# One stretch of attention products per tile in a linear-attention, GLU and expert kernel, with the routing's counting products ahead of every third one

## The chip, the cores and the metric

The kernel runs on one core of one Trainium2 chip. The metric is the device time of one execution in microseconds (us). PE is TensorE, DVE is VectorE, ACT is ScalarE, POOL is GpSimd, SP is SyncE.

## What is computed

Three layers follow one another over 3072 tokens (4 sequences of 768) of 384 columns, all in float32: linear attention with 8 heads of 48 columns and a decay per column, a gated unit (GLU) behind a norm, and a layer of 8 experts of which each token takes one.

```python
def _attn_ref(q, k, v, alpha):                     # [4, 8, 768, 48]
    state = np.zeros((B, H, D, D), dtype=np.float32)
    for t in range(S):
        state = alpha[:, :, t, :, None] * state + np.einsum('bhd,bhe->bhde', k[:, :, t], v[:, :, t])
        y[:, :, t] = np.einsum('bhd,bhde->bhe', q[:, :, t], state)
...
def _moe_ref(x, w_gate, w_val, w_out, rms_g):      # d_ff = 1536
    xn = x / np.sqrt(np.mean(x * x, axis=-1, keepdims=True) + 1e-06) * rms_g
    g = xn @ w_gate
    return (g * (1.0 / (1.0 + np.exp(-g))) * (xn @ w_val)) @ w_out
...
def _moe2_ref(x, w_gate, w_output_gate, w1, w2):   # 8 experts, F = 1024
    logits = x @ w_gate
    e_idx = np.argmax(logits, axis=1)
...
        out[mask] = gate_w[mask, None] * eom[mask, e, None] * (np.maximum(x[mask] @ w1[e], 0.0) @ w2[e])
```

## The kernel before

**Tiles and groups.** The tokens are cut into 24 tiles of 128. Tiles 0 to 17 take turns over the first three sequences, 18 to 23 are the fourth sequence; tiles 15, 16, 17 and 23 are the last of their sequence and have no state product, and 18 is the first of its own: it has no product with an older state. Three tiles make a group g of the GLU, eight groups in all.

**The GLU** runs per group over 12 chunks j of 128 hidden columns, in slots: gate (`m_gate`, L635), val (`m_val`, L654) and, one chunk behind, out (`m_out`, L676), nine matmuls each, since every float32 product is made of three. ACT and DVE work between them: `tt` is the activated gate times val (L661; it frees val's bank of PSUM), `hh` its rounded part (L664, ACT), `hl` the rest (L670, DVE). The next slots of the out kind need `hh` and `hl`.

**Attention of one tile** has five stages (`stages`, L415): score (L430, two banks `ps_s`, for even and for odd heads; behind it DVE makes the masked P, L440, and decays the state, L434), k turned, output (L464 with the older state `wide`, L468 with P), state (L489; DVE adds it to the state, L496), x turned. From tile 9 on (`DT`) it is `moved(t)` (L910) that arranges them: the turns of k and x go through DVE transposes (L557, L510) and DMAs in place of PE, and PE has two visits per tile, the score, and two slots' groups later output and state together (`yd_`, L918). A stage is called behind a slot by `stage()` (L951), when the condition at L1287 says that it is due. What a tile needs ahead of its score (transposes of alpha, k and q, two scans, two multiplications) is its preparation, `prework(t)` (L366), which is queued in `prep` and taken a step per slot.

**The banks.** The attention and the routing take their PSUM banks from one pool, `psA`, with three buffers (L160); the slots have five others. `bank()` (L231) takes the next buffer of the pool, and PE waits until the one that it held last is read.

**The normed output.** ACT squares the output and sums it (L474), POOL makes the scale `ss` of the sum (L475, L476), ACT scales (`xn`, L477), DVE turns it (`xb`, L510).

**Routing** of a group's 384 tokens to experts has two halves: `route_a` (L709), some twenty small operations, mostly DVE's, and `route_b` (L744), six small bf16 products that count tokens per expert (`ps_r`, L748 to L752), a few DVE operations (the two that read the counts are L760 and L767), and three scatters of rows to the experts' buckets, issued by POOL (L769). They are called at fixed slots of the next group, L1292 to L1297.

**What sets the order.** On PE the groups 2 to 6 run in program order (`seq`, L215). The other engines' instructions are put in order by a scheduler at build time, save for the few that are pinned. Each engine works through its own list in that order.

The preparation begins at stage 0 of a tile, ahead of its score:

```python
        if done % NST == 0:
            while prep:
                prep_step()
            if nprep < NTILE and done != GS - NST:
                prep.extend(prework(nprep))
                nprep += 1
```

## Time and profile before

| | before |
|---|---|
| median of 3 runs | 822.46 us (822.12 to 822.76) |
| the profiled execution, its own time | 821.73 us |
| its span | 819.9 us |
| PE, busy | 804.4 us (98%) |
| VectorE, busy | 539.0 us (66%) |
| ScalarE, busy | 326.3 us (40%) |
| POOL, busy | 153.8 us (19%) |
| mean granted clock of TensorE | 0.998 |

The rows come from one profiled execution. Its span is the time from the first to the last instruction in the trace; 1.83 us lie around it, and its own time is 0.73 us below the median of the runs. In the rows, the start of a PE instruction is the number to use: durations of matmuls overlap, so that what a matmul takes is the time from its start to the next one's. The same holds in a smaller degree for VectorE. Times in brackets at a row's end are idle time of that engine ahead of it, and what ended it.

### The profile page before, as it was taken

Reading aid. Unit: us, or ns where it says so; the run is one execution under the profiler, and the core shown is the slowest. Engines: PE = TensorE matmul, PEld = TensorE weight load, DVE = VectorE, ACT = ScalarE, POOL = GpSimd, SP = SyncE. Lnnn points to the kernel's source line nnn. Section 1 sums busy time; section 2 is a strip of 40 time slices with the busy share of each in tenths; the row PEclk is TensorE's granted clock in tenths of the full one; section 3 lists DMA queues with packets and bytes.
Section 4 is the critical chain, followed back from the end, with each engine's and each line's share of the span. In section 5 each row is a group of like instructions: output and inputs, shape, how many; then the busy total and the mean of one; then the engine's idle time right before and its main releaser. Section 6 shows DMA issues by size and latency. Waiting matters only on the chain.

```text
span 819.9 us, 15933 instructions
## 1 busy us (share of the span) xinstructions
PE 804.4 (98%) x5967; PEld 772.2 (94%) x5967; DVE 539.0 (66%) x1202; ACT 326.3 (40%) x694; POOL 153.8 (19%) x207
## 2 busy tenths in 40 slices
PE   7999999999999999999999999999999999999996
PEld 5799999999999999999999999999999999999996
DVE  7998999498677876766776663243357555566631
ACT  1745554333333333422433332325226445554441
POOL 3001000000300020010020001001224325544441
PEclk9999999999999999999999999999999999999999
DMA  9955463773544453334444221005037786778620
GB/s 202 208 155 144 153 170 111 219 181 84 149 111 102 108 137 82 83 97 93 108 119 101 49 47 49 20 9 195 1 116 203 201 223 186 218 233 254 177 86 27
DMA packets 195454, 106.85 MB, mean 130 GB/s; under 512 B 125868, under 2 KB 190122, under 8 KB 195376
## 3 DMA queue, kind: packets, MB, share of 16 engines
q1 hardware_dynamic: 190912, 96.35, 46.1%
q0 software_dynamic: 4464, 9.48, 3.4%
q8 instruction: 47, 0.77, 0.4%
q14 instruction: 31, 0.25, 0.1%
HBM read 80.88 MB, written 25.18 MB: 129 GB/s over the span
## 4 chain that ended last, share of the span: by engine, by line
PE 94%; issue 2%; DVE 1%; DMA 1%; POOL 1%; ACT 0%; POOLq 0%; DVEq 0%; ACTq 0%; SPq 0%
PE ps_o L684 19%; PE ps_g L650 19%; PE ps_v L650 18%; PE ps_h L650 12%; PE ps_b L1196 8%; PE ps_b L1202 4%; PE ps_s L430 3%; PE ps_y L468 3%; PE ps_y L464 2%; PE ps_st L489 1%; PE pc L615 1%; PE ps_n L283 1%; PE junk L860 1%; PE ps_k L450 1%; DMA er<-bucket 0%
## 5 line engine op out<-in xcount | busy, mean ns | idle before, releaser
L664 ACT ACTIVATE hh<-tt 128x384 fp32r<-128x384 f32 x96 | 50.4, 525 | 145.3 <-DVE tt L661 134.8
L661 DVE TENSOR_TENSOR tt<-tt,ps_v 128x384 f32<-128x384 f32 x96 | 52.8, 550 | 82.2 <-PE ps_v L650 69.5
L1176 DVE SCALAR_TENSOR_TENSOR h<-ps_h,h 128x256 fp32r<-128x256 f32 (+6 forms) x72 | 38.1, 532 | 63.5 <-ACT h L1175 60.3
L642 ACT ACTIVATE tt<-ps_g 128x384 f32<-128x384 f32 x96 | 46.9, 488 | 82.8 <-PE ps_g L650 76.9
L670 DVE TENSOR_TENSOR hl<-tt,hh 128x384 fp32r<-128x384 f32 x96 | 54.2, 565 | 24.1 <-ACT hh L664 22.6
L650 PE MATMUL ps_g<-xh,wgh 128*128 128x384 f32 x192 | 66.5, 346 | 0.0
L650 PE MATMUL ps_v<-xh,wvh 128*128 128x384 f32 x192 | 66.4, 346 | 0.0
L684 PE MATMUL ps_o<-wol,hh 128*128 128x400 f32 x192 | 66.3, 345 | 0.0
L650 PE MATMUL ps_g<-xl,wgh 128*128 128x384 f32 x192 | 64.6, 337 | 0.8 <-DVE begin L317 0.8
L684 PE MATMUL ps_o<-woh,hh 128*128 128x400 f32 x192 | 65.3, 349 | 0.0
L650 PE MATMUL ps_v<-xh,wvl 128*128 128x384 f32 x192 | 64.8, 338 | 0.0
L650 PE MATMUL ps_g<-xh,wgl 128*128 128x384 f32 x192 | 64.6, 337 | 0.0
L650 PE MATMUL ps_v<-xl,wvh 128*128 128x384 f32 x192 | 64.5, 336 | 0.0
L684 PE MATMUL ps_o<-woh,hl 128*128 128x400 f32 x192 | 64.0, 345 | 0.0
L1175 ACT ACTIVATE h<-ps_h 128x256 fp32r<-128x256 f32 (+6 forms) x72 | 33.5, 468 | 71.6 <-PE ps_h L650 69.9
L650 PE MATMUL ps_h<-x,w1b 128*128 128x456 f32 (+3 forms) x288 | 57.5, 342 | 0.0
L650 PE MATMUL ps_h<-x,w1a 128*128 128x256 f32 (+3 forms) x288 | 52.2, 325 | 0.0
L650 PEld LDWEIGHTS ps_h<-x,w1b 128*128 128x128 f32 x288 | 50.6, 188 | 1.7 <-ACT x L1156 0.2
L650 PEld LDWEIGHTS ps_h<-x,w1a 128*128 128x128 f32 x288 | 47.2, 188 | 1.0 <-issue 0.3
L440 DVE TENSOR_TENSOR P<-ps_s,mask 128x512 f32<-128x512 f32 x46 | 30.1, 685 | 23.8 <-PE ps_s L430 23.8
L475 POOL TENSOR_SCALAR ss<-ss 128x1 f32<-128x1 f32 x24 | 9.8, 410 | 186.4 <-ACT xn L474 183.1
L1196 PE MATMUL ps_b<-h,w2b 128*128 128x456 f32 (+2 forms) x216 | 43.6, 344 | 0.3 <-ACT h L1175 0.3
(312 smaller groups left out, 2027.3 us busy)
## 6 DMA issues: line engine op xcount, KB each, us to landing
st<-in_moe_w_dram SPq DMA_DIRECT2D x46, 384.0 KB
bucket<-zero SPq DMA_DIRECT2D x8, 772.0 KB
stg<-in_moe_w_gate_dram SPq DMA_DIRECT2D x12, 384.0 KB
stg<-in_moe_w_val_dram SPq DMA_DIRECT2D x12, 384.0 KB
stg<-in_moe_w_out_dram SPq DMA_DIRECT2D x12, 384.0 KB
v<-in_v_dram SPq DMA_DIRECT2D x23, 192.0 KB
more<-in_moe_w_dram SPq DMA_DIRECT2D x9, 384.0 KB
er<-in_moe_w_dram SPq DMA_DIRECT2D x9, 384.0 KB
```

The source lines that it names most:

```text
L430: seq(nc.tensor.matmul(ps[hh][:, p, :], lhsT=kT[r, p, :], rhs=qT[r, p, :], start=True, stop=True))
L440: pace(f'Ph{t}', nc.vector.tensor_tensor(out=Ph, in0=ps[hh], in1=mb, op=ALU.mult))
L642: nc.scalar.activation(tt, ps, AF.Silu)
L650: seq(nc.tensor.matmul(ps, lhsT=a_[:, kc, :], rhs=b_[:, kc, :], start=(n == 0), stop=(n == 3 * KD - 1)))
L661: nc.vector.tensor_tensor(out=tt, in0=tt, in1=ps, op=ALU.mult)
L664: nc.scalar.activation(hh, tt, AF.Copy)
L670: nc.vector.tensor_tensor(out=hl, in0=tt, in1=f(hh), op=ALU.subtract)
L684: seq(nc.tensor.matmul(obank[s][i], lhsT=a_[:, sl], rhs=weight(b_, j), start=(j == j0 and n == 0), stop=(j == j1 - 1 and n == 2)))
L1175: nc.scalar.activation(hh[:, 0, :], ps, AF.Relu)
L1176: nc.vector.scalar_tensor_tensor(out=hh[:, 1, :], in0=ps, scalar=0.0, in1=f(hh[:, 0, :]), op0=ALU.max, op1=ALU.subtract)
L1196: nc.tensor.matmul(ob2[u][k_][:, 0:r * n], lhsT=we[p][b_][:, j, k_ * P:k_ * P + P], rhs=hh[:, a_, :], start=(j == 0 and m == 0), stop=(j = ...
L1202: ins = nc.tensor.matmul(ob2[u][i][0:r], lhsT=hh[:, a_, sl], rhs=we[p][b_][:, j, :], start=(j == 0 and m == 0), stop=(j == KF2 - 1 and m = ...
```

## The change

From tile 9 on the state's products come first, then the output's, and behind them, in the same stage, the score of the next tile, whose `stages` are made there (`scored`). What is left of the next tile's preparation is issued ahead of that. The score stage of these tiles is empty (`no_`), save for tile 9, whose score still stands alone. A tile's preparation is queued one stage earlier, at the last stage of the tile before it.

The second half of the routing, up to group 5, is called directly ahead of such a stretch, at the first one behind its first half: at the tiles 10, 11, 14, 17, 20 and 23. Its two reads of the counts (`counts`) stand ahead of the arithmetic of the gates. The first half lies at slot 4 (group 0), 15 (group 1) or 12 of the next group, where it lay at 1 and 7. Groups 6 and 7 are as before.

```diff
@@ -752,19 +752,26 @@
         seq(nc.tensor.matmul(ps[:, GT, :], lhsT=ones_b, rhs=ohc[:, GT - 1, :], start=True, stop=True))
         bc = [P, GT, E]
 
+        rk = small("rk", bc)
+
+        def counts():
+            nc.vector.tensor_tensor(out=rk, in0=ps[:, 0:GT, :], in1=cnt.to_broadcast(bc), op=ALU.add)
+            nc.vector.tensor_tensor(out=cnt[:, 0, :], in0=cnt[:, 0, :], in1=ps[:, GT, :], op=ALU.add)
+
+        if g < NG - 1:
+            counts()
         nc.vector.tensor_scalar(out=se, in0=se, scalar1=1e-9, scalar2=2.0, op0=ALU.add, op1=ALU.mult)
         nc.vector.reciprocal(out=se, in_=se)
         nc.vector.scalar_tensor_tensor(out=R[:, :, DM:DM + 1], in0=og, scalar=1.0, in1=se, op0=ALU.add, op1=ALU.mult)
         nc.vector.tensor_copy(R[:, :, DM + 1:DM + 2], tokid[:, g * GT:g * GT + GT, :])
-        rk = small("rk", bc)
-        nc.vector.tensor_tensor(out=rk, in0=ps[:, 0:GT, :], in1=cnt.to_broadcast(bc), op=ALU.add)
+        if g == NG - 1:
+            counts()
         nc.vector.tensor_tensor(out=rk, in0=rk, in1=oh, op=ALU.mult)
         pf = small("pf", [P, GT, 1])
         nc.vector.tensor_reduce(out=pf, in_=rk, op=ALU.add, axis=AX.X)
         nc.vector.tensor_scalar(out=m8, in0=m8, scalar1=-float(REG), scalar2=float(E * REG), op0=ALU.mult, op1=ALU.add)
         pos = small("pos", [P, GT, 1], I32)
         nc.vector.tensor_tensor(out=pos, in0=pf, in1=m8, op=ALU.add)
-        nc.vector.tensor_tensor(out=cnt[:, 0, :], in0=cnt[:, 0, :], in1=ps[:, GT, :], op=ALU.add)
         for i in range(GT):
             nc.gpsimd.indirect_dma_start(out=bucket_of[g * GT + i], out_offset=OFF(ap=pos[:, i, 0:1], axis=0),
                                          in_=R[:, i, 0:RW], in_offset=None)
@@ -907,8 +914,10 @@
     DT = CFG['DT']
     laid = []
 
+    scored = {}
+
     def moved(t):
-        s_, k_, y_, d_, _ = stages(t)
+        s_, k_, y_, d_, _ = scored.pop(t) if t in scored else stages(t)
 
         def second():
             if t == DT:
@@ -916,7 +925,12 @@
             return laid.pop() if laid else None
 
         def yd_():
-            posts = [y_(), d_()]
+            posts = [d_(), y_()]
+            if t + 1 < NTILE:
+                while prep:
+                    prep_step()
+                scored[t + 1] = list(stages(t + 1))
+                posts.append(scored[t + 1][0]())
 
             def post():
                 for p in posts:
@@ -934,7 +948,7 @@
 
         def no_():
             return None
-        return s_, second, yd_, turns, no_
+        return s_ if t == DT else no_, second, yd_, turns, no_
 
     def rest():
         yield lambda: None
@@ -950,12 +964,14 @@
 
     def stage():
         nonlocal done, nprep
-        if done % NST == 0:
+        t_, i_ = divmod(done, NST)
+        t_ += GT
+        if i_ == 0 and t_ <= DT:
             while prep:
                 prep_step()
-            if nprep < NTILE and done != GS - NST:
-                prep.extend(prework(nprep))
-                nprep += 1
+        if nprep < NTILE and ((i_ == 0 and t_ < DT and done != GS - NST) or (i_ == NST - 1 and t_ >= DT - 1)):
+            prep.extend(prework(nprep))
+            nprep += 1
         done += 1
         return next(att_stream)()
 
@@ -1285,15 +1301,18 @@
             if post:
                 post()
             if done < (NTILE - GT) * NST + 2 and ((g - 1) * 3 * KF + n + 1 + lead(g, n)) * GT >= (done + 1 - GT * NST) * 3 * KF / NST:
+                if done % NST == 2 and not last:
+                    for g_ in [*rt]:
+                        route_b(g_)
                 post = stage()
                 if post:
                     post()
             prep_step()
-            if g == 2 and n in (1, 3):
-                (route_a, route_b)[n // 2](0)
-            if n == CFG['RA']:
+            if g == 2 and n == 4:
+                route_a(0)
+            if n == (CFG['RA'] if last else 15 if g == 2 else 12):
                 route_a(g - 1)
-            if n == CFG['RB']:
+            if last and n == CFG['RB']:
                 route_b(g - 1)
             if last:
                 if n == 9:
```

On PE, around the output of tile 12, before: output (`ps_y`), state (`ps_st`), then an out slot.

```order
L650 MATMUL ps_v<-xl,wvhe 128x384
L650 MATMUL ps_v<-xh,wvle 128x384
L464 MATMUL ps_y<-wide_127,qT 64x96 x8
L468 MATMUL ps_y<-v,P_3321 64x48 x8
L468 MATMUL ps_y<-v,P_3323 64x48 x8
L489 MATMUL ps_st<-v,kn 64x48 x8
L684 MATMUL ps_o<-wohe,hh 128x400
L684 MATMUL ps_o<-wole,hh 128x400
```

The score of tile 13 stood alone, between a val and an out slot further on:

```order
L650 MATMUL ps_v<-xh,wvh 128x384
L650 MATMUL ps_v<-xl,wvh 128x384
L650 MATMUL ps_v<-xh,wvl 128x384
L430 MATMUL ps_s<-qT,kT 128x128 x8
L684 MATMUL ps_o<-woh,hh 128x400
L684 MATMUL ps_o<-wol,hh 128x400
L684 MATMUL ps_o<-woh,hl 128x400
```

And in the changed kernel, at the place of the first of the two:

```order
L650 MATMUL ps_v<-xl,wvhe 128x384
L650 MATMUL ps_v<-xh,wvle 128x384
L489 MATMUL ps_st<-v,kn 64x48 x8
L464 MATMUL ps_y<-wide_127,qT 64x96 x8
L468 MATMUL ps_y<-v,P_3214 64x48 x8
L468 MATMUL ps_y<-v,P_3216 64x48 x8
L430 MATMUL ps_s<-qT,kT 128x128 x8
L684 MATMUL ps_o<-wohe,hh 128x400
L684 MATMUL ps_o<-wole,hh 128x400
```

The state's products have moved ahead of the output's, and the score of tile 13 from its own boundary to directly behind them.

On VectorE, around the addition of tile 10's state (`state_125`), before. `tt` is the instruction that frees val's bank.

```order
L670 TENSOR_TENSOR hl<-tt,hh 128x384
L527 TENSOR_TENSOR xl<-xn,xh 128x3x128
L387 STREAM_TRANSPOSE qT<-blk_q 128x4x4x32
L496 TENSOR_TENSOR state_125<-ps_st,state_125 128x192
L411 TENSOR_TENSOR kT<-kT,Z 128x512
L661 TENSOR_TENSOR tt<-tt,ps_v 128x384
L411 TENSOR_TENSOR qT<-qT,aT 128x512
L670 TENSOR_TENSOR hl<-tt,hh 128x384
L510 STREAM_TRANSPOSE xb<-xn 128x3x4x32
```

And in the changed kernel, where the counts `ps_r` of group 0 are read here too:

```order
L527 TENSOR_TENSOR xl<-xn,xh 128x3x128
L411 TENSOR_TENSOR qT<-qT,aT 128x512
L758 TENSOR_TENSOR rk<-ps_r,cnt 128x24
L496 TENSOR_TENSOR state_125<-ps_st,state_125 128x192
L387 STREAM_TRANSPOSE aT<-blk_a 128x4x4x32
L759 TENSOR_TENSOR cnt<-cnt,ps_r 128x8
L769 TENSOR_TENSOR rk<-rk,oh 128x24
L387 STREAM_TRANSPOSE qT<-blk_q 128x4x4x32
L315 COPY en<-aT 128x4
L771 TENSOR_REDUCE pf<-rk 128x3
L718 TENSOR_SCALAR oh<-ex 128x24
```

The addition stands now among the reads of the counts, two transposes of the next tile's preparation and the two halves of a routing; the next `tt` is 32 rows behind it, where it was two.

On POOL, around the scatters of group 4 (`bucket`), before: behind `ss` of tile 19 and ahead of the preparation of a later tile (`Z`) and of `ss` of tile 20.

```order
L406 MEMSET Z 128x1
L475 TENSOR_SCALAR ss<-ss 128x1
L476 TENSOR_TENSOR ss<-ss,mhalf 128x1
L769 DMA bucket<-R,pos 26624x386 x3
L406 MEMSET Z 128x1
L475 TENSOR_SCALAR ss<-ss 128x1
L476 TENSOR_TENSOR ss<-ss,mhalf 128x1
L406 MEMSET Z 128x1
```

And in the changed kernel:

```order
L406 MEMSET Z 128x1
L475 TENSOR_SCALAR ss<-ss 128x1
L476 TENSOR_TENSOR ss<-ss,mhalf 128x1
L406 MEMSET Z 128x1
L776 DMA bucket<-R,pos 26624x386 x3
L475 TENSOR_SCALAR ss<-ss 128x1
L476 TENSOR_TENSOR ss<-ss,mhalf 128x1
L406 MEMSET Z 128x1
```

The scatters have moved behind the memset of `Z`. The counts that they need come from products between the tiles 19 and 20 before, and from the stretch of tile 20 itself after, the one whose `ss` is next in this list.

## Rows read from the trace of the kernel before

**Rows 1.** The page's first part: busy us (share) and instructions by engine.

```profile
PE 804.4 (98%) x5967; PEld 772.2 (94%) x5967; DVE 539.0 (66%) x1202; ACT 326.3 (40%) x694; POOL 153.8 (19%) x207
```

**Rows 2.** PE in time, a lone score: start, duration, line, operation, tiles, count.

```profile
341.16 0.34 PE L650 MATMUL ps_g<-xl,wgh 128*128 128x384 f32 x1
341.33 0.34 PE L650 MATMUL ps_g<-xh,wgl 128*128 128x384 f32 x1
341.60 1.16 PE L430 MATMUL ps_s<-qT,kT 48*128 48x128 f32 x16
342.69 0.45 PE L650 MATMUL ps_v<-xh,wvh 128*128 128x384 f32 x1
342.98 0.34 PE L650 MATMUL ps_v<-xl,wvh 128*128 128x384 f32 x1
```

**Rows 3.** PE in order of time, output and state products of one tile.

```profile
440.82 0.88 PE L464 MATMUL ps_y<-wide,qT 128*64 128x96 f32 x16
441.53 1.09 PE L468 MATMUL ps_y<-v,P 128*64 128x48 f32 x32
442.45 0.64 PE L489 MATMUL ps_st<-v,kn 128*64 128x48 f32 x16
```

**Rows 4.** PE in order of time, at the kernel's start.

```profile
14.73 0.67 PE L468 MATMUL ps_y<-v,P 128*64 128x48 f32 x16
15.34 1.16 PE L430 MATMUL ps_s<-qT,kT 48*128 48x128 f32 x8
...
17.01 0.67 PE L468 MATMUL ps_y<-v,P 128*64 128x48 f32 x16
17.61 0.66 PE L283 MATMUL ps_n<-ident,nat 128*128 128x128 f32 x4
```

**Rows 5.** PE in order of time, counting products alone in a boundary.

```profile
204.57 0.34 PE L650 MATMUL ps_g<-xh,wgl 128*128 128x384 f32 x1
204.75 0.18 PE L748 MATMUL ps_r<-ohb,tri_b 128*128 128x8 bf16 x1
...
205.17 0.33 PE L650 MATMUL ps_v<-xl,wvh 128*128 128x384 f32 x1
```

**Rows 6.** VectorE in order of time, counts and transposes.

```profile
216.60 0.18 DVE L761 TENSOR_TENSOR rk<-rk,oh 128x24 f32<-128x24 f32 x1
216.70 0.15 DVE L767 TENSOR_TENSOR cnt<-cnt,ps_r 128x8 f32<-128x8 f32 x1
...
226.68 0.85 DVE L510 STREAM_TRANSPOSE xb<-xn 128x384 f32<-128x384 f32 x1
227.45 1.06 DVE L557 STREAM_TRANSPOSE kb<-kT 128x512 f32<-128x512 f32 x1
228.44 1.05 DVE L387 STREAM_TRANSPOSE aT<-blk_a 128x512 f32<-128x512 f32 x1
```

**Rows 7.** By line, 200 to 500 us: count, busy us, mean ns, idle before.

```profile
L661 DVE TENSOR_TENSOR tt<-tt,ps_v 128x384 f32<-128x384 f32 x52 | 28.5, 548 | 30.9 <-PE ps_v L650 25.7 <-issue 2.9 <-ACT tt L642 2.2
...
L440 DVE TENSOR_TENSOR P<-ps_s,mask 128x512 f32<-128x512 f32 x26 | 16.9, 686 | 16.8 <-PE ps_s L430 16.8
...
L318 DVE TENSOR_TENSOR_SCAN Z<-aT,begin 128x511 f32<-128x511 f32 x12 | 14.7, 1222 | 0.3
...
L477 ACT ACTIVATE xn<-ps_y,ss 128x384 f32<-128x384 f32 x14 | 8.1, 581 | 17.6 <-POOL ss L476 15.9 <-POOL Z L406 1.7
...
L496 DVE TENSOR_TENSOR state<-ps_st,state 128x192 f32<-128x192 f32 x10 | 3.5, 355 | 3.7 <-PE ps_st L489 3.7
```

**Rows 8.** POOL in order of time, `ss` and the scatters.

```profile
353.57 0.19 POOL L475 TENSOR_SCALAR ss<-ss 128x1 f32<-128x1 f32 x1 [2.85 <-ACT xn L474]
353.84 0.55 POOL L476 TENSOR_TENSOR ss<-ss,mhalf 128x1 f32<-128x1 f32 x1
...
359.36 0.96 POOL L769 DMA_INDIRECT bucket<-R,pos  x1 [0.30 <-issue]
360.62 0.96 POOL L769 DMA_INDIRECT bucket<-R,pos  x1 [0.31 <-issue]
```

## The prediction

> **What bounds the kernel now.** I read the totals first. In the profiled execution PE is busy for 804.4 of 819.9 us, VectorE for 539, ScalarE for 326 [rows 1]. So time is gained or lost here only where PE's own instructions get shorter or where PE starts to wait. The reader is to see that no other engine is full, but that VectorE is the one that could become late: it is at two thirds over all, and at more around the tiles.
>
> Then I read PE's instructions in order of time at the places that the change touches. Within a slot one matmul of 384 columns follows the other after 0.17 us [rows 2]. Between two slots stands a visit to attention. The score alone: 341.33 to 341.60 is 0.27 us from the last full matmul to the first score, that is 0.10 more than the spacing; and 342.69 to 342.98 is 0.29 from the first full matmul behind it to the second, 0.12 more [rows 2]. The rows name no wait of PE there. So a visit costs, beside its products, about 0.21 us: 0.10 for going in and 0.11 for coming back.
>
> **The change: visits joined.** From tile 9 on the score of tile t+1 stands directly behind the output of tile t, so the tiles 10 to 23 lose a visit each: 14. A visit of its own costs an entry and a return, 0.21 us. What the joined order has instead is one change inside the stretch, from P products (128x64) to scores (48x128). The start of the kernel shows it: 16 P products followed by scores take 14.73 to 15.34, 0.61 us; followed by full transposes they take 17.01 to 17.61, 0.60 us [rows 4]. Leaving P for the scores so costs what leaving it for a full tile costs, which the old order paid as well. I take the whole 0.21, 14 x 0.21 = 2.9 us. Ends: P followed by state products takes 441.53 to 442.45, 0.92 us for 32 [rows 3], so nothing in these rows lets a change be cheaper than free; if it were free I would gain some 0.10 more each, 4.3 us; if it cost an entry and a return, nothing.
>
> The Trainium skill, page "TensorEngine Tiling (Array Packing)", section "Key Properties", says that changing the tiling mode, not just the tile, drains TensorE. By that rule each of the old four changes per tile (into and out of either visit) has its price and the new order still has three of them; a quarter of the two visits' 0.42 us would be 0.10 a tile, 1.5 us in all instead of 2.9, an estimate from that page. The two rows of 0.61 and 0.60 us speak for the larger figure, since they show no price for the scores above that for a full tile.
>
> **Counting products.** Alone in a boundary they take, from the full matmul ahead to the second one behind, 204.57 to 205.17, 0.60 us, where two spacings would be 0.35: 0.25 each [rows 5]. Before, five of the six groups up to tile 23 stand so and one behind a stretch; after, six stand ahead of a stretch, whose entry is there anyway. No row shows that; it costs between nothing and the 0.25 of standing alone. I take 0.18, nearer to the latter since the six products have to run in any case, and a gain of 0.3 us (0 to 0.5, lest they overlap more than I think). What else is moved (the preparation of a tile begins one stage earlier, the first half of a routing lies in later slots) issues the same instructions, none of them on PE.
>
> **New waits.** A stretch of state, output and two scores needs four banks of a pool of three, five with the counting products. So the second score bank waits for VectorE's addition that frees the state bank, and with a route the first one waits for VectorE's `cnt`. From the state products to the second score PE has 0.71 + 0.92 us of other products as cover [rows 3]; the addition takes 0.36 [rows 7] and is hidden unless a long instruction is ahead of it: a transpose of 1.05 us [rows 6] or a scan of 1.22 [rows 7]. At tiles 9, 11 and 14 one is. I take 0.3 for the three together (0 to 1.0).
>
> Tile 10. Here VectorE has both a second and a first half of a routing, two scans, two transposes and the two P ahead of the `tt` that frees the val bank. From the stretch's start S the addition can begin at S + 0.9 (six counting products and the state's, 0.8, and the release). Then, by duration: addition and decay of the state 0.7, two scans 2.4, two P 1.4 [rows 7], two transposes 2.1 [rows 6], together 6.6; each starts some 0.08 ahead of its predecessor's end (226.68 to 227.45 is 0.77 for one of 0.85 [rows 6]), so 6.0; and 22 small ones at 0.10 (216.60 to 216.70 [rows 6]), 2.2. `tt` starts at S + 9.1 and frees the bank 0.55 [rows 7] and a release later, S + 9.75. PE wants it after the stretch (counts 0.16, state 0.46 as half of P's 0.92, `wide` 0.71, P 0.92 and 0.10 for leaving, scores 1.09 as in [rows 2]: 3.4), val (1.56), out (1.64) and gate (1.56), nine matmuls each: S + 8.2, or 8.35 with the return. **1.4 us**, ends 0 and 2.0. Before, the pieces lay at four boundaries, and VectorE had its gaps between them.
>
> Tiles 20 and 17. In either order POOL has the three bucket scatters of a group between the `ss` of two tiles; but the counts now come from the second one's own stretch, so the scatters are issued just when that tile's `ss` is wanted, where they had half a tile's time to themselves. A scatter takes 1.26 us from start to start, `ss` 0.82 in all [rows 8]. ScalarE's `xn` waits for `ss`, VectorE's `xb` for `xn`, and `kb` and the `hl` that the out slot needs are queued behind `xb`. Tile 20: `pos` at S + 4.2 (counts, addition, a scan, a transpose), scatters 3.8, `ss` 0.8, `xn` 0.6 [rows 7], `xb` 0.8, `kb` 1.0 [rows 6], `hl` 0.6: S + 12.0 at the earliest. The out slot's first `hl` product is due after the stretch, five slots (7.9) and two matmuls, S + 11.7. With releases between four engines, I take **0.9 us** (0 to 1.2). Tile 17 has a second transpose of q ahead of its `tt`, which waits for the reload of the block that the first one has read. No row of before shows that wait; between nothing and the 1.4 of tile 10, I take **0.5**, nearer to nothing since the slot wants `tt` only five slots later. At tiles 12, 13, 19, 21 and 22, without a route, I find no wait, since the addition has only a `tt` or `hl` (0.5) ahead of it. The transfers of x and k start earlier or up to 4 us later, and are wanted a whole tile (some 20 us) later; nothing.
>
> Sum: -2.9 - 0.3 + 0.3 + 1.4 + 0.9 + 0.5 = -0.1 us. The profiled execution took 821.73 us (span 819.9 and 1.8 around it), so 821.6; it lies 0.73 below the median of the three runs, 822.46, against which the result is held: **822.4 us**. What a measurement of this kernel can tell from no change is about 0.2%, 1.6 us.
>
> **Rivals.** (a) The waits are hidden and the joins pay in full. For it: VectorE is busy for only two thirds [rows 1], the small instructions of tile 10 may overlap, and every wait above is an estimate with zero as its end. Against it: four banks asked of three is no estimate, and the batch of tile 10 is longer than its cover by any of my sums. With waits of 0.5 us in all: -3.2 + 0.5 = -2.7, 819.8 us.
>
> (b) Slower: the scatters hold up `ss` at all the routed stretches as at tile 20. For it: at all six the scatters stand directly ahead of the `ss` of their stretch's tile. It decides from the point at which `pos` comes later than S + 4 us, when `hl` comes later than the out slot's S + 11.7. Against it: at tiles 11 and 14 the transpose of q or a scan stands behind `pos` and not ahead. Price: 0.6 more at four of them, +2.4, so +2.3 and 824.8 us.
>
> (c) Joining gives less, since the change inside the stretch has a price of its own: at a gain of 0.10 each instead of 0.21 the sum is +1.4, 823.9 us, still within what is not told from no change.
>
> (d) The change doesn't do what it says: scores that wait so long for the second bank that the stretch is broken open at every tile. PE would stand 0.3 us at each of 14, +4.2 - 0.1, 826.6 us. The cover of 1.6 us against an addition of 0.3 speaks against it.
>
> **How the numbers follow.** My forecast, together with (c), within 0.2%: 0.45. (a), faster: 0.33. (b) 0.18 and (d) 0.04, slower: 0.22. The range takes in (a) and most of (b): from -2.9, the joins in full with almost no wait, 819.6, to +2.5, 825.0. Outside are joins at their upper end with no wait, and (d). The likeliest case's own range is 820.9 to 824.1.
>
> **What would show it.** In the trace after: one entry and one return per tile from tile 10 on, P to score 1.02 us for 32 products, and the sum of the visits some 0.2 us shorter per tile. Idle time of PE ahead of val just behind tile 10's stretch (some 1.4 us, released by `tt`), ahead of an out matmul behind tiles 17 and 20 (released by `hl`), and little ahead of the scores. If the idle time ahead of val is missing, (a) holds; if `hl` holds up the out slots of tiles 11, 14 and 23 too, (b). The forecast would be wrong altogether if PE showed a lower granted clock after than before, which nothing here points to, or if the time moved in the part behind attention, whose instructions stand in the same order.

## The result: slower by half a per cent

| | before | after |
|---|---|---|
| median of 9 runs each, us | 822.76 (821.97 to 829.38) | 826.94 (825.02 to 828.47) |
| profiled execution, us | 821.73 | 826.31 |
| its span, us | 819.9 | 824.5 |
| between the two marks below, us | 309.02 | 312.15 |

The ratio is 1.0051, with an interval of 1.0036 to 1.0066: the changed kernel is slower by 4.2 us (3.0 to 5.4). Forecast was 822.4 us, with a range from 819.6 to 825.0; the time lies above the range.

To see where the time went I set two marks in PE's order, between which all the joined stretches lie: the val slot behind the lone score of tile 9, and a val slot behind the place where the lone score of tile 23 stood. First the kernel before, PE in order of time (start, duration, line, operation):

```profile
197.03 0.45 PE L650 MATMUL ps_v<-xh,wvh 128*128 128x384 f32 x1
...
506.05 0.34 PE L650 MATMUL ps_v<-xh,wvh 128*128 128x384 f32 x1
```

The same two matmuls in the changed kernel:

```profile
196.58 0.45 PE L650 MATMUL ps_v<-xh,wvh 128*128 128x384 f32 x1
...
508.73 0.34 PE L650 MATMUL ps_v<-xh,wvh 128*128 128x384 f32 x1
```

That is 309.02 us before and 312.15 after, 3.13 more. A second execution of each was traced in the course of the experiments: before took 309.02 again, after took 314.14, 5.12 more. So the attention part of before repeats to the hundredth, and the two values of after lie on both sides of the 4.2 us of the medians. Outside the marks the times vary from execution to execution in before itself (the second trace of before has a span of 821.6, 1.7 us more than the first, with nothing of it between the marks). I compare between the marks from here on.

### The profile page after: what moved, and what is told of

It is laid out like the page before. It is cut to its first block, busy times and chain, and to the rows that moved or that the text cites. A ratio compares the mean times of both kernels' runs of the same rounds, so it can differ in the third digit from the quotient of the medians.

```text
span 824.5 us, 15944 instructions
## 1 busy us (share of the span) xinstructions
PE 803.3 (97%) x5967; PEld 773.2 (94%) x5967; DVE 533.5 (65%) x1202; ACT 326.8 (40%) x694; POOL 152.2 (18%) x207
## 4 chain that ended last, share of the span: by engine, by line
PE 78%; DMA 7%; issue 4%; DVE 4%; POOL 2%; SPq 2%; ACT 2%; POOLq 0%; DVEq 0%; ACTq 0%
PE ps_o L684 17%; PE ps_g L650 16%; PE ps_v L650 16%; PE ps_h L650 8%; PE ps_b L1212 4%; PE ps_b L1218 3%; PE ps_s L430 3%; PE ps_y L468 2%; PE ps_y L464 2%; PE ps_st L489 1%; POOL bucket L776 1%; PE pc L615 1%; DMA er<-bucket 1%; DMA st<-in_moe_w_dram 1%; DMA nat<-in_k_dram 1%
## 5 line engine op out<-in xcount | busy, mean ns | idle before, releaser
L776 POOL DMA_INDIRECT bucket<-R,pos x24 | 26.8, 1116 | 135.4 <-issue 41.3
L406 POOL MEMSET Z<- 128x1 f32 x19 | 1.9, 102 | 213.5 <-DVE kT L411 213.5
```

The lines of the kernel that those rows point to most:

```text
L776: nc.gpsimd.indirect_dma_start(out=bucket_of[g * GT + i], out_offset=OFF(ap=pos[:, i, 0:1], axis=0), in_=R[:, i, 0:RW], in_offset=None)
```

## The profile after

The page's first part, to be held against [rows 1]: PE has the same number of instructions and is busy for 1.1 us less, and yet the span is longer. PE now waits.

```profile
PE 803.3 (97%) x5967; PEld 773.2 (94%) x5967; DVE 533.5 (65%) x1202; ACT 326.8 (40%) x694; POOL 152.2 (18%) x207
```

What PE waited for between 197 and 509 us (line, what ended the wait: us in total, times, longest). The same view of before is empty. The view names 3.8 us; the lengths of the slots, in the table below, show more.

```profile
PE ps_st L489 <- DMA kn<-mid_k: 1.8, 2, 1.6
PE ps_v L650 <- DVE tt L661: 1.8, 2, 1.1
PE ps_o L684 <- DVE hl L670: 0.2, 1, 0.2
```

**The joined stretch itself does what it should.** Tile 19 has no route; PE in order of time, the answer to [rows 2] and [rows 3]:

```profile
421.13 0.34 PE L684 MATMUL ps_o<-woh,hl 128*128 128x400 f32 x1
421.40 0.67 PE L489 MATMUL ps_st<-v,kn 128*64 128x48 f32 x16
421.90 0.85 PE L464 MATMUL ps_y<-wide,qT 128*64 128x96 f32 x16
422.58 1.09 PE L468 MATMUL ps_y<-v,P 128*64 128x48 f32 x32
423.60 1.16 PE L430 MATMUL ps_s<-qT,kT 48*128 48x128 f32 x16
424.69 0.45 PE L650 MATMUL ps_g<-xh,wgh 128*128 128x384 f32 x1
424.97 0.34 PE L650 MATMUL ps_g<-xl,wgh 128*128 128x384 f32 x1
```

One entry (421.13 to 421.40, 0.27), one return (424.69 to 424.97, 0.28), and from P to the scores 1.02 us for 32 products. The boundary has become 1.09 us longer than in before (5.02 instead of 3.93 from the last slot's first matmul to the next one's), and where the score stood alone 1.18 and 0.12 us are gone: a gain of 0.21 us, at every tile from 10 to 23.

**Where it was lost.** Lengths of PE's slots, from first matmul to first matmul, after less before, and less what the join and the counting products make (a stretch without any wait is +1.09, with the counting products ahead of it +1.24):

| part | us |
|---|---|
| 14 joins of 0.21 | -2.94 |
| counting products: six groups that stood alone (five) or behind a stretch (one), -0.16 to -0.26 each; five ahead of a stretch, +0.15 each (the sixth, at tile 23, lies behind the second mark) | -0.68 |
| tiles 9, 11, 14: scores wait for the second bank, 0.21 + 0.55 + 0.03 | +0.79 |
| tile 10: val waits for `tt` | +0.93 |
| tile 10: behind that the out slot waits for `hl` and the next val for `tt`, both late because ScalarE stands at `xn` until `ss` comes | +0.65 |
| tiles 11 and 12: state products wait for `kn`, 0.26 + 1.66 | +1.92 |
| tiles 11 and 20: out slot waits for `hl`, 0.50 + 0.30 | +0.80 |
| tile 17: val waits for `tt`, which is behind the second transpose of q | +1.63 |
| sum | +3.10 (measured 3.13) |

The largest is one that the prediction had at nothing. Its chain begins at tile 11, all engines in order of time (an entry in brackets is the engine's idle time ahead of the instruction, and what ended it):

```profile
243.77 0.88 PE L464 MATMUL ps_y<-wide,qT 128*64 128x96 f32 x16
...
246.09 1.09 DVE L387 STREAM_TRANSPOSE qT<-blk_q 128x512 f32<-128x512 f32 x1
247.01 0.16 DVE L774 TENSOR_TENSOR pos<-pf,m 128x3 int32<-128x3 f32 x1
...
247.29 1.23 DVE L328 TENSOR_TENSOR_SCAN aT<-aT,begin 128x512 f32<-128x512 f32 x1
...
247.49 1.91 POOL L776 DMA_INDIRECT bucket<-R,pos  x1 [5.70 <-DVE state L434]
...
249.70 0.96 POOL L776 DMA_INDIRECT bucket<-R,pos  x1 [0.30 <-issue]
...
250.97 0.96 POOL L776 DMA_INDIRECT bucket<-R,pos  x1 [0.30 <-issue]
...
252.00 0.19 POOL L475 TENSOR_SCALAR ss<-ss 128x1 f32<-128x1 f32 x1
...
252.87 0.58 ACT L477 ACTIVATE xn<-ps_y,ss 128x384 f32<-128x384 f32 x1 [3.46 <-POOL ss L476]
...
253.49 0.88 DVE L510 STREAM_TRANSPOSE xb<-xn 128x384 f32<-128x384 f32 x1 [2.37 <-ACT xn L477]
...
254.29 1.04 DVE L557 STREAM_TRANSPOSE kb<-kT 128x512 f32<-128x512 f32 x1
...
255.25 0.51 DVE L670 TENSOR_TENSOR hl<-tt,hh 128x384 fp32r<-128x384 f32 x1
...
263.41 0.34 SPq L564 DMA_DIRECT2D kn<-mid_k  x1
...
266.85 0.67 PE L489 MATMUL ps_st<-v,kn 128*64 128x48 f32 x16 [1.59 <-DMA kn<-mid_k]
```

The reader is to see one line of dependence through five engines. `pos` stands behind a transpose of q. The three scatters stand ahead of `ss` in POOL's order and keep POOL from 247.49 to 252.00. ScalarE, which idles for 3.46 us, then makes `xn`, and VectorE, idle for 2.37, transposes it into `xb`. Only behind that comes `kb`, though k has nothing to do with `ss`. Its way through DRAM ends at 266.85, 12.6 us after its transpose began, and there the next stretch begins with the state's products, which need it. The output started at 243.77, so `kn` was issued 19.6 us behind that. The same places in the kernel before:

```profile
242.07 0.88 PE L464 MATMUL ps_y<-wide,qT 128*64 128x96 f32 x16
...
249.03 0.87 DVE L510 STREAM_TRANSPOSE xb<-xn 128x384 f32<-128x384 f32 x1
...
257.94 0.35 SPq L564 DMA_DIRECT2D kn<-mid_k  x1
...
263.19 0.88 PE L464 MATMUL ps_y<-wide,qT 128*64 128x96 f32 x16
...
264.82 0.64 PE L489 MATMUL ps_st<-v,kn 128*64 128x48 f32 x16
```

There it is 257.94 less 242.07, 15.9 us, and the state's products stood behind the output's, at 264.82 with the output at 263.19: 1.6 us more of time. Of the 3.8 us by which `kn` is issued later, 2.8 are there when `xb` starts (9.7 us behind the output's start against 7.0). The other 1.0 comes behind `kb` in SP's queue, where the second half of k's way stands behind the load of `xn`: that load is issued 3.1 us after the stores of x have all been issued (260.00 against 256.93), in before 1.6 us (254.04 against 252.47). What joining takes from `kn` on the one side and the scatters add on the other is more than it had to spare.

Tile 17 is another path. VectorE, and PE behind it:

```profile
378.13 1.07 DVE L387 STREAM_TRANSPOSE qT<-blk_q 128x512 f32<-128x512 f32 x1
...
384.80 1.08 DVE L387 STREAM_TRANSPOSE qT<-blk_q 128x512 f32<-128x512 f32 x1 [4.18 <-DMA blk_q<-in_q_dram]
...
385.73 0.54 DVE L661 TENSOR_TENSOR tt<-tt,ps_v 128x384 f32<-128x384 f32 x1
...
386.33 0.45 PE L650 MATMUL ps_v<-xh,wvhe 128*128 128x384 f32 x1 [1.09 <-DVE tt L661]
```

The block is reloaded after the first transpose has read it, and VectorE, with `tt` queued behind, stands 4.18 us for it. The three scatters are issued at 379.71, 381.08 and 382.35, in just this time.

## The experiments

Three theories stood at the start. **S:** the scatters, which now come just when the same tile's `ss` is wanted, hold up `xn`, `xb`, `kb` and `hl`, and so `kn`. **B:** PE waits for banks that VectorE frees late, since the routing lies in its batch, whatever POOL does. **J:** the joined stretch itself makes the waits, through its banks and the order in it. All times between the marks stand against 309.02 of before. Ratios are to the kernel before on the same chip. Diffs are against the changed kernel unless they say otherwise.

**e1: scatters behind `ss`.** POOL's order is changed: the scatters of a group (now in a function `scatter`) are issued one slot later, and the `ss` of the stretch's tile is kept ahead of them. In the traces PE and VectorE have the same order as in the changed kernel, up to the experts; on ScalarE `xn` has moved forward at five tiles.

```diff
-                pace(f'ss{t}', nc.gpsimd.tensor_tensor(out=ss, in0=ss, in1=mhalf, op=ALU.pow))
+                ins = nc.gpsimd.tensor_tensor(out=ss, in0=ss, in1=mhalf, op=ALU.pow)
+                if t >= CFG['DT']:
+                    tc.keep_in_program_order(ins)
+                else:
+                    pace(f'ss{t}', ins)
...
+        if g < NG - 2:
+            held.append([1, scatter])
+        else:
+            scatter()
```

> The changed kernel, but POOL issues the three scatters of a group behind the two ss operations of the tile in whose stretch the counts stand, not ahead of them (both pinned in that order); nothing else moves. Theory S (the scatters hold up ss, and with it xn, xb, kb, the k transfer and hl): the waits of PE for ps_g behind tile 10 (0.3), for hl behind tiles 11 and 20 (0.5 and 0.3) and for kn ahead of tile 12 (1.6) go, some 2.7 to 3.3 us, so about 823.5 us. Theory B (the waits are those for banks that VectorE frees, whatever POOL does): less than 0.6 us is gained, about 826.5 us.

Measured: 1.0018 (1.0003 to 1.0033), and 309.16 between the marks: 2.99 us of the 3.13 are gone (by the ratios, 1.0018 against 1.0051, some 2.7 us). At tile 11, POOL and VectorE:

```profile
247.11 0.19 POOL L475 TENSOR_SCALAR ss<-ss 128x1 f32<-128x1 f32 x1 [4.47 <-ACT xn L474]
...
251.92 0.87 DVE L514 STREAM_TRANSPOSE xb<-xn 128x384 f32<-128x384 f32 x1
```

`xb` no longer waits, and there is no wait for `kn` or `hl` left; tile 10's 0.65 behind ScalarE is gone too. What stays is 0.2 at tile 9, the 0.9 at tile 10, 0.7 at tile 11's scores, and tile 17, a little worse (2.0 us). S is right for about 3 us of the 6.7 us of waits, and not for the rest.

**e2: joins alone.** The routing is back in its old slots.

```diff
-                if done % NST == 2 and not last:
-                    for g_ in [*rt]:
-                        route_b(g_)
...
-            if g == 2 and n == 4:
-                route_a(0)
-            if n == (CFG['RA'] if last else 15 if g == 2 else 12):
+            if g == 2 and n in (1, 3):
+                (route_a, route_b)[n // 2](0)
+            if n == CFG['RA']:
                 route_a(g - 1)
-            if last and n == CFG['RB']:
+            if n == CFG['RB']:
                 route_b(g - 1)
```

> The stretches of the changed kernel (state, output, next score), but both halves of the routing at the slots of the kernel before, the counting products in boundaries of their own. Theory S and theory B alike: without the routing at the stretch VectorE's batch is short and POOL is free, so most of the 6.7 us of waits go and the joins' 2.9 us stand: 820.0 to 821.0 us, faster than before. Theory J (the joined stretch itself brings the waits: the state's products ask for kn earlier, q is reloaded later): 823 us or more, no faster than before.

Measured: 1.0009 (0.9996 to 1.0023); between the marks 310.63, 1.61 more than before. The waits of the changed kernel at tiles 10, 12, 17 and 20 are gone, but twice the counting products fall directly or one slot behind a joined stretch and wait for the bank of the output, which ScalarE's `xn` frees. PE:

```profile
288.80 0.17 PE L748 MATMUL ps_r<-ohb,tri_b 128*128 128x8 bf16 x1 [1.24 <-ACT xn L477]
...
288.95 0.50 PE L650 MATMUL ps_v<-xh,wvh 128*128 128x384 f32 x1
289.25 0.52 PE L650 MATMUL ps_v<-xl,wvh 128*128 128x384 f32 x1
289.57 0.52 PE L650 MATMUL ps_v<-xh,wvl 128*128 128x384 f32 x1
```

The second price shows in the spacing behind the wait, 0.32 us instead of 0.17. By stretches (length, busy us of the engines, then PE's granted clock, share of the DMA engines, GB/s):

```profile
288.00:289.00 1.00, 0.20 (x7) 0.20 (x6) 1.00 (x2) 0.58 (x1) 0.13 (x1) 1.00 0.71 185
289.00:292.50 3.50, 3.50 (x16) 3.49 (x13) 2.56 (x10) 0.00 (x0) 0.88 (x1) 0.52 0.74 170
292.50:300.00 7.50, 7.50 (x44) 7.50 (x43) 4.69 (x7) 1.54 (x3) 2.12 (x3) 1.00 0.50 126
```

Behind the wait the granted clock is at the lower of its two levels, 1.2 GHz, which made the next two slots 1.21 and 0.34 us longer: 1.55 us for a wait of 1.24. The forecast of S and B, 820 to 821 us, is missed; the time is the one that J gave, no faster than before, but most of it goes to these two places and not to the stretch. I had missed that two of the old places of the routing don't suit the joined order either; they lie too close behind a stretch.

**e3: routing alone.** The visits are separate again, as before; the routing stays where the change has put it.

```diff
-            posts = [d_(), y_()]
-            if t + 1 < NTILE:
-                while prep:
-                    prep_step()
-                scored[t + 1] = list(stages(t + 1))
-                posts.append(scored[t + 1][0]())
+            posts = [y_(), d_()]
...
-        return s_ if t == DT else no_, second, yd_, turns, no_
+        return s_, second, yd_, turns, no_
```

> The routing of the changed kernel (first halves later, counting products directly ahead of the visit of output and state), but the visits as before: output, state, and the score alone. Theory S: the scatters stand ahead of ss here too, so the waits for ps_g, hl come back: 824 to 826 us. Theory B: with one bank less asked for by a visit nothing waits: 822.5 us, and 0.3 less for the counting products' entry. Theory J: 822.5 us as well.

Measured: 1.0004 (0.9991 to 1.0017); between the marks 308.93, 0.09 less than before, with no wait of PE named. What the counting products gain is nearly lost again in two out slots, behind the tiles 11 and 17, that are 0.23 and 0.36 us longer than in before. The scatters are ahead of `ss` here too, but VectorE has `pos` ahead of the transpose of q, not behind it:

```profile
244.14 0.16 DVE L774 TENSOR_TENSOR pos<-pf,m 128x3 int32<-128x3 f32 x1
244.31 1.10 DVE L387 STREAM_TRANSPOSE qT<-blk_q 128x512 f32<-128x512 f32 x1
...
250.68 0.86 DVE L510 STREAM_TRANSPOSE xb<-xn 128x384 f32<-128x384 f32 x1 [0.57 <-ACT xn L477]
```

`xb` starts 8.2 us behind the output's start (242.47) where it was 9.7 in the changed kernel and 7.0 in before, and `kn` is wanted 1.6 us later than in a joined stretch. So neither half of the change is slow alone between the marks (this one 0.09 less, the joins' 1.61 more mostly through two old places); both together are. The forecast of S, 824 to 826 us with the waits back, was wrong, and S needs a correction. As I read the rows, the scatters hurt because the joined order has the preparation of the next tile ahead of `pos`, and wants `kn` first; the two were not varied apart.

**e4: k ahead of x.** If `kn` is late because `kb` stands behind `xb`, k could be sent first.

```diff
         def turns():
+            if t + 1 < NTILE and place_of[t + 1][1] < NCH - 1:
+                turn_k(t + 1)
             moves[t][0]()
...
-            if t + 1 < NTILE and place_of[t + 1][1] < NCH - 1:
-                turn_k(t + 1)
```

> The changed kernel, but the turn of the next tile's k (kb and its transfers) is issued ahead of the turn of x, so that kn lands some 3 us earlier and doesn't hang on xn. Theory S and theory J: the wait for kn ahead of tile 12 (1.6) and tile 11 (0.3) goes, the waits for hl and ps_g stay: about 825 us. If kn is late for another reason (the transfer itself): no change, 826.9 us.

Measured: 1.0381 (1.0367 to 1.0394), 854.78 us where about 825 was expected; between the marks 337.92, 28.90 more than before. The `kn` waits are gone, and others come in their place; what PE waited for between 197 and 509 us, the first two:

```profile
PE ps_s L430 <- DVE rk L769: 10.0, 4, 4.8
PE ps_s L430 <- DVE state L496: 5.2, 4, 1.7
```

x's way through DRAM starts later, an instruction of VectorE that needs x waits for it (7.78 us at one place), and the counts, the state and the banks stand behind that. The rows of this kernel also show four stretches at the lower clock between the marks. So x, sent behind k, has even less time to spare than k, and I looked for the fix where the delay comes from.

**e5 and e6: routing half-way, and joins only from tile 12.** In e5 the second half of a routing is called at the first stage of a tile instead of the third, and the first half in its old slot; e6 is e5 with the visits joined only from the output of tile 12 on. `r_after_again` is the changed kernel once more on the same chip.

```diff
-                if done % NST == 2 and not last:
+                if done % NST == 0 and not last:
...
-            if g == 2 and n == 4:
+            if g == 2 and n == 1:
                 route_a(0)
-            if n == (CFG['RA'] if last else 15 if g == 2 else 12):
+            if n == CFG['RA']:
```

> The stretches of the changed kernel at all tiles from 9 on, but the counting products half-way between two stretches (at the first stage of a tile), first halves of the routing where the kernel before has them. Theory S and B (what costs is the routing at or right behind a stretch: its scatters ahead of ss, its VectorE operations in the batch, its bank taken from the output): no wait is left but 0.2 us at tile 9 and up to 0.6 at tile 11, so -2.9 + 0.8 = 2.1 us faster than the kernel before on the same chip, ratio 0.9975. Theory J (joining the state's products, output and score brings waits by itself): at best as fast as before, ratio 1.000 or more.

> As the run with the counts between the stretches, but joined only from tile 12 on (scores of tiles 13 to 23: 11 joins); tiles 9 to 11 have two visits as in the kernel before. Theory S and B: no wait, -11 x 0.21 = 2.3 us against before, ratio 0.9972. Theory J: ratio 1.000 or more.

> The changed kernel once more, on the chip of the two runs above. Every theory: ratio 1.004 to 1.006 to the kernel before, its waits for kn ahead of tile 12, for tt behind tiles 10 and 17 and for hl behind tile 11 as in its first trace.

Measured: 1.0052 (1.0033 to 1.0072), 1.0056 (1.0035 to 1.0076) and, for the changed kernel, 1.0051 (1.0033 to 1.0069); between the marks +3.25, +4.36 and +5.12. e5 and e6 missed what S and B gave, for a reason beside the point: groups 0 and 1 now meet in one slot, the second one's counting products wait for VectorE, which has the chains of both in a row, and behind that wait the granted clock is at the lower level (0.57 from 216 to 219.5 us). PE in e5:

```profile
215.84 0.18 PE L748 MATMUL ps_r<-ohb,tri_b 128*128 128x8 bf16 x1 [1.90 <-DVE ohb L730]
```

The two slots there are 2.9 and 1.5 us longer than in the changed kernel. From tile 15 on e5 has no wait at all and gains 0.21 per tile, so the half-way place itself is good. Of the changed kernel the second trace shows the same waits, but 1.84 us for `tt` at tile 17, and behind it

```profile
387.00:391.00 4.00, 3.93 (x13) 3.93 (x14) 3.81 (x6) 0.96 (x3) 0.00 (x0) 0.57 0.48 106
391.00:400.00 9.00, 9.00 (x53) 9.00 (x52) 4.30 (x7) 3.40 (x8) 0.10 (x1) 1.00 0.61 136
```

the clock at the lower level, which makes the slot 1.31 us longer than in the first trace. That and the longer wait (0.75) are 2.06 us, which is what lies between the two traces of after (1.99).

**e7 and e8: three slots ahead of a stretch.** Groups 0 and 1 are in their old slots, groups 2 to 5 at the second stage of a tile; e8 is e7 with joins only from tile 12.

```diff
-                if done % NST == 2 and not last:
+                if done % NST == 1 and g > 2 and not last:
...
-            if n == (CFG['RA'] if last else 15 if g == 2 else 12):
+            if n == CFG['RA']:
                 route_a(g - 1)
-            if last and n == CFG['RB']:
+            if (last or g == 2) and n == CFG['RB']:
```

> Joined stretches at all tiles from 9 on; the counting products of groups 0 and 1 at the slots of the kernel before, those of groups 2 to 5 some three slots ahead of a stretch (at the second stage of a tile, when the k transfer of that tile is over), alone in a boundary. Theory S and B: what cost 4 us in the run with the counts between the stretches was the two routings called at once, so here no wait is left but 0.2 at tile 9 and 0.6 at tile 11: ratio 0.9975 (0.9965 to 0.9985). Theory J: ratio 1.000 or more, with waits at most stretches.

> The same, joined only from tile 12 on: 11 joins, tiles 9 to 11 as before. Theory S and B: no wait, -2.3 us, ratio 0.9972. Theory J: 1.000 or more.

Measured: 1.0002 (0.9990 to 1.0013) and 1.0002 (0.9988 to 1.0016), both above what S and B gave; between the marks +0.43 and -0.48. In e7 the waits for `kn` are gone, and tile 17 loses 0.9 instead of 1.6, but the counting products stand alone again, and tile 14 loses 1.3 us at its scores, of which 0.57 is named as a wait for the addition of the state; tile 20 loses 0.4.

**e9 and e10: three to four slots behind a stretch.** The second half of groups 2 to 5 is called behind slot 12, the rest as in e7; e10 again with joins only from tile 12.

```diff
-                if done % NST == 2 and not last:
-                    for g_ in [*rt]:
-                        route_b(g_)
...
-            if last and n == CFG['RB']:
+            if n == (CFG['RB'] if last or g == 2 else 12):
                 route_b(g - 1)
```

> Joined stretches at all tiles from 9 on; the routing of groups 0 and 1 as in the kernel before, the counting products of groups 2 to 5 three to four slots behind a stretch and eight ahead of the next, alone in a boundary: far enough from the output's bank behind, and from ss, tt and the second score bank ahead. Theory S and B (the price is in what the routing meets on VectorE, POOL and in the banks): between tiles 9 and 23 only 0.2 us (tile 9) and 0.6 (tile 11) are lost, and 14 x 0.21 = 2.9 gained, some 2.1 us in the trace between 197 and 506 us, ratio 0.9975 (0.996 to 0.999). Theory J (the stretch itself waits): some 0.5 us or more are lost at most tiles, ratio 1.000 or more.

> The same, joined only from tile 12 on, 11 joins, no tile with a wait by theory S and B: -2.3 us in the trace between 197 and 506 us, ratio 0.9972 (0.996 to 0.999). Theory J: 1.000 or more.

> The kernel before once more, with a trace, to see how much its parts ahead of 197 us and behind 506 us differ from execution to execution. Every theory: between 197 and 506 us no wait of PE and the same times as in the first trace within 0.1 us; the first matmuls of the experts (some 613 us) and the stretch about 760 us later by 1 to 5 us in most executions, since runs of this kernel lie between 822 and 826 us.

Measured: 0.9988 (0.9972 to 1.0005) for e9, 822.26 us against 824.45 of before on that chip, and 0.9993 (0.9978 to 1.0007) for e10; between the marks -1.50 and -1.40, and 0.00 for before. In e9 no wait of PE is named between 197 and 509; tiles 9, 11 and 14 lose 0.21, 0.58 and 0.63 at the scores. S and B had -2.1 for e9; tile 14 is the one that they had not. So J is worth 1.4 us, half of what the joins gain, and what is left of the changed kernel's 6.7 us of waits, 5.3, comes of where the routing stands in the joined order. The 0.9 at tile 10, which e1 left, is gone in e2 and e9: it was the routing in VectorE's batch, as B has it. e9 is the best of the kernels run: a gain that the trace shows and the times can't tell from no change.

**Tile 17.** The traces also bear on why the reload of q is slow, without a run of its own. The second transpose of q starts 6.7 us after the first in after, 7.0 in e1, 6.1 in e7, 4.6 in e9 and 4.9 in e2. It waits for the last of the four pieces of the block. SP issues that piece at these times, in the changed kernel, in e9 and in e7:

```profile
381.17 0.46 SPq L263 DMA_DIRECT2D blk_q<-in_q_dram  x1
...
378.04 0.43 SPq L263 DMA_DIRECT2D blk_q<-in_q_dram  x1
...
380.77 0.43 SPq L263 DMA_DIRECT2D blk_q<-in_q_dram  x1
```

The first transposes start at 378.13, 375.64 and 377.28, so it is 3.04, 2.40 and 3.49 us. The rest is the landing. The transfers of `blk_q` around it (shortest, median, longest time to landing), in the changed kernel and then in e9; the longest in after, and 2.2 in e9, is this piece:

```profile
DMA to landing us min/median/max: 1.9/2.0/3.6
```

```profile
DMA to landing us min/median/max: 1.9/2.2/2.5
```

So of the 2.07 us by which after is slower here than e9, 1.43 lie in the landing and 0.64 in SP's queue, where the load of `v` (379.58) stands between the first piece and the others; in e9 it is issued ahead of the first transpose. With scatters in the same microseconds the longest landing is 3.6 us (4.0 in e1), without them 2.5 (2.7 in e2 and e7); between 381 and 383 us the changed kernel's DMA engines are at a share of 1.02. In e7 the last scatter was issued at 374.23, the piece lands in 2.6, and still tile 17 loses 0.9; `v` stands there too, for 0.90 us. So the scatters are not the whole reason. That they, and not another difference between the kernels, make the landing later is what the rows suggest, and was not varied by itself.

## Why the prediction was wrong

**The joins: right.** -2.9 was forecast, from rows at the kernel's start, and -2.94 came, 0.21 at each of 14 tiles. The rule of the Trainium skill, page "TensorEngine Tiling (Array Packing)", section "Key Properties", that a change of tiling mode drains TensorE, was weighed there at 0.10 a tile; 0.21 decides against that reading of it, and rival (c) falls.

**Counting products: right in kind, too small.** -0.68 between the marks, and with the sixth stretch, at tile 23, which lies behind the second mark and costs 0.15 as well, -0.53 against -0.3; that is at the upper end of the 0 to 0.5. Ahead of a stretch they cost 0.15, less than the 0.18 that I took, and taking away an old place gave up to 0.26.

**"The transfers of x and k start earlier or up to 4 us later, and are wanted a whole tile (some 20 us) later; nothing": the step that failed first.** k started 3.8 us later (19.6 against 15.9), as the sentence allows, but nearly the whole tile is what the way takes: `kb`, two legs through DRAM and the queue in SP need it to within a few us. I never subtracted arrival from demand, and demand had moved forward by 1.6 us, because the state's products had moved to the head of the stretch. PE waited 1.92 us for `kn` where the sum has nothing, and with it the statement that tile 12 has no wait is wrong.

**Rival (b) was the true mechanism, and its price is right by luck.** "At tiles 11 and 14 the transpose of q or a scan stands behind `pos` and not ahead" was the argument against it. The rows of after show one scan and the transpose ahead of `pos` at both tiles (at tile 11 a scan at 244.46, the transpose at 246.09, `pos` at 247.01) and only the second scan behind it. By the rival's own mark, `pos` later than 4 us behind the stretch's start, tile 11 (4.3) had to be late and tile 14 (3.5) not, and so it came: of the tiles 11, 14 and 23, which were named as the sign, only the out slot of 11 waited for `hl`. Its price of 0.6 each counted `hl`, of which 0.80 was measured in all, and left out `kn` (1.92) and ScalarE at tile 10 (0.65): together 3.37 us. That the forecast's 0.9 for tile 20 and the rival's 2.4 more come to 3.3 is luck.

**Tile 10: the size right by luck.** 1.4 was forecast for VectorE's batch ahead of `tt`, and that measured 0.93. Another 0.65 came through `ss` and ScalarE, which was not in the sum; only the two together, 1.58, are near it.

**Tile 17: the wait found, mis-sized.** 0.5 taken, 1.63 measured. The upper end of 1.4 was taken from tile 10's batch, a length that has nothing to do with a reload. It should have been worked out from the transfer: one transpose, the place in SP's queue, landing.

**Tile 20: oversized.** 0.9 taken, 0.30 measured. The chain came out as it was worked out: from the stretch's start at 443.86, `pos` at 447.95 (4.1, forecast 4.2) and `hl` ready at 455.87 (12.0, forecast 12.0), against a need at 11.7. The terms written down add up to 11.8 and not to 12.0, so some 0.2 went to the releases between engines, and not the 0.6 that I had added for them.

**Second bank: 0.79 for tiles 9, 11 and 14, against 0.3,** within its ends of 0 to 1.0. Rival (d) falls: scores wait at three tiles, not at all.

In sum: gains of -3.62 against -3.2, waits of +6.72 against +3.1. More than half of the error between the marks (1.92 of 3.2 us) is one omission, that what a delayed `ss` holds up includes the way of k. The median lies 4.5 us above the forecast; the 1.3 that are left lie outside the marks or in the difference between executions of after (1.99 between the two traced), and no run takes them apart.

## What to carry to other kernels

When pieces of work are joined, the gain at the joint can be read off rows exactly; the risk lies in what the moved pieces need. For each product that moves forward, subtract the arrival of its latest operand from its new place, through every queue on the way, before calling a transfer covered. And look at what is queued ahead of a small but urgent instruction on an otherwise idle engine: three scatters on POOL, which is busy for 18% of the span, delayed four other engines.

## What the runs showed of the hardware

A scatter that POOL begins while VectorE is in a scan takes longer: 1.90 to 1.94 us for the first scatters at the tiles 10, 11 and 14, 1.37 for the second at tile 10, which begins 0.6 us into its scan. They end 0.8 to 1.0 us after the scan. Those at the tiles 17 and 20, beside no scan, take 0.96 to 1.07. Before has it too (1.72 at 290.12, 1.39 at 426.97). At tile 11 above, the scan runs from 247.29 to 248.52 and the scatter ends at 249.40. The Trainium skill, page "SBUF — State Buffer", section "Who interferes with whom", says that a VectorE instruction with two inputs in SBUF contends with a GpSimd instruction that reads SBUF; these rows agree with it, a scan of `aT` with `begin` against a scatter that reads `R` and `pos`. It lengthens the chain to `ss` by some 0.9 us at the tiles 11 and 14, and by 1.4 at tile 10.

A wait of PE can have a second price. Behind waits of 1.24 us (e2), 1.84 (the second trace of after) and 1.90 (e5) the granted clock was at 1.2 GHz (0.52 to 0.57 in the stretches read), which cost PE some 1.3 to 1.6 us each; behind waits of 1.59 us (tile 12) and 1.45 (tile 17 in e1) it stayed at 2.4 GHz. In before and e9, which don't let PE wait there, it never fell between the marks. The same happens outside them, in some executions: in e1 the granted clock is 0.51 from 21.5 to 25.0 us, where in after it is 1.00, and the first GLU matmul starts at 36.54 instead of 35.01. So a trace's whole span holds more than the change, which is why the stretch between two marks was compared.
